# Weight slots of 6176 instead of 6144 bytes, weights 16 bytes inside, state-and-value tiles of 3328 instead of 3200 bytes

## The chip, the core and the metric

The kernel runs on one core of one Trainium2 chip. The metric is the device time of one execution in microseconds (us); a nanosecond is written ns. Engines are named as the profile names them: PE is the matrix engine (its matmuls), PEld its weight loads, DVE the vector engine, ACT the scalar engine, POOL the general one, and SP the engine that issues the DMAs.

## What is computed

A recurrent attention layer (4 batches, 8 heads, 768 steps, head size 48), and two MLPs behind it, all in float32:

```python
f = 1.0 / (1.0 + np.exp(-f_logit))
for t in range(S):
    state = f[:, :, t, :, None] * state + np.einsum('bhd,bhe->bhde', k[:, :, t], v[:, :, t])
    y[:, :, t] = np.einsum('bhd,bhde->bhe', q[:, :, t], state)
...
x = attn_out.transpose(0, 2, 1, 3).reshape(3072, 384)
h = x @ w_in;  g = np.maximum(h, 0.0) ** 2;                     x = g @ w_out     # first MLP, 384 -> 2048 -> 384
h = x @ w_in2; g = h * np.tanh(np.log1p(np.exp(h)));            return g @ w_out2 # second MLP, same sizes
```

## The kernel before

**Tiling.** The 3072 tokens are six blocks of 512. The hidden size of 2048 is sixteen chunks of 128, numbered fc. For each MLP and each block, `l1` (matmul at line 333) computes the hidden activations of one chunk and `l2` (line 344) adds that chunk's share to three accumulators. Each is a group of nine matmuls of 128x128 weights against 512 columns: three 128-column slices of the weights, times three products (high part of the weights with the high and the low part of the activations, low part of the weights with the high part). Every matmul of a group uses weights other than the one before it, so each has its own weight load (LDWEIGHTS). Six blocks, two MLPs, sixteen chunks and two projections make 384 groups, that is 3456 matmuls of 512 columns; the very last group is issued as 18 half-width matmuls by `last_l2` (line 840).

**Stages.** First comes a start of some 34 us with attention work alone. Then the first MLP runs with the attention of the later token blocks interleaved in PE's queue (short matmuls at lines 471, 486, 518, 525, 538 and others). From about 425 us on, PE does only the second MLP. In both MLPs PE's queue alternates the groups: `l1` of chunk fc, then `l2` of a chunk one or two back, then `l1` of the next. The order of the first part is written out in a table (`START`), and the rest by due times (`put`); neither is touched.

**Where the weights lie.** A weight tile holds, in each of 128 partitions, 1536 floats (6144 bytes): two halves (for `l1` and for `l2`), in each a high and a low part of 384 floats. All slices of 128 columns begin at multiples of 512 bytes inside the tile. Sixteen such slots, tags `w_0` to `w_15` of pool `wp`, hold the first MLP's weights: `load_w` (line 240) fetches the packed float64 bits into the slot, DVE and ACT take them apart into a `wbit` tile, and `w_hi` and `w_lo` (lines 275 and 281) write the high and low parts back into the slot. The first four of these slots in memory, `w_15` to `w_12`, serve earlier as input tiles of the attention (`early`). The second MLP's weights go through DRAM: `w2_back` (line 316) fetches chunks 5 to 15 into `w_0` to `w_10`, and chunk 4 into a slot `w_late` of pool `at2`; `w2_early` fetches the two halves of chunks 0 to 3 into tiles of the attention that are free by then (pool `lt`; table `EARLY`): the `l1` halves into `kn0`, `kn1`, `mv0`, `mv1`, the `l2` halves into `vs0` to `vs3`, the state-and-value tiles.

Tiles follow one another in memory by their sizes, in the order in which the pools are opened and the tags first used. That gives each tile's place in its partition; what is left over modulo 256 bytes is, before and after:

| tile | place modulo 256, before | after |
|---|---|---|
| weights in slots, in memory order `w_15`, `w_14`, `w_13`, `w_12`, `w_0` ... `w_9`, `w_11`, `w_10` | all 0 | 16, 48, 80, 112, 144, 176, 208, 240, and the same eight again |
| chunk 4 of the second MLP (`w_late`) | 0 | 16 |
| `l1` halves of chunks 0 to 3, second MLP (`kn`, `mv`) | all 0 | all 0 |
| `l2` halves of chunks 0 to 3, second MLP (`vs0` to `vs3`) | 0, 128, 0, 128 | all 0 |
| activations `x`, `gh`, `gl` (the moving operand of every group) | all 0 | all 0 |
| attention inputs `early` (begin of slots `w_15` to `w_12`) and `in` | 0 and 128 | 0, 32, 64, 96 and 128 |

Of the kernel before, what the change touches and what calls it, by code (L numbers as in the profile page):

```python
# [9 lines left out]
F32 = mybir.dt.float32  # L10
F32R = mybir.dt.float32r
U32 = mybir.dt.uint32
# [17 lines left out]
DM = 384  # L30
# [53 lines left out]
@with_exitstack  # L84
def attention_mlps(ctx: ExitStack, tc: tile.TileContext, qkf, vv, w1, w2, out):
    keep = ctx.enter_context(tc.tile_pool(name="keep", bufs=1))
    flag = keep.tile([1, 1], I32, name="flag")
    fast_path(tc, flag, qkf, vv, w1, w2, out)
    beyond = tc.nc.values_load(flag[0:1, 0:1], min_val=0, max_val=1)
    with tc.If(beyond > 0):  # L90
        stepwise_path(tc, qkf, vv, (w1, w2), out)
# [122 lines left out]
def fast_path(ctx: ExitStack, tc: tile.TileContext, flag, qkf, vv, w1, w2, out):  # L214
    nc = tc.nc
    V, A, G, T = nc.vector, nc.scalar, nc.gpsimd, nc.tensor
    const = ctx.enter_context(tc.tile_pool(name="const", bufs=1))
    wp = ctx.enter_context(tc.tile_pool(name="wp", bufs=1))
    bit_p = ctx.enter_context(tc.tile_pool(name="bit", bufs=3))
    lt = ctx.enter_context(tc.tile_pool(name="lt", bufs=1))  # L220
# [17 lines left out]
    xt, wt, raw, bits, hps, gt, accs, x2t = {}, {}, {}, {}, {}, {}, {}, {}  # L238

    def load_w(fc):  # L240
        t = wp.tile([128, 2 * DM, 2], U32, tag=f"w_{fc}", name=f"r_{fc}", bufs=1)
        nc.sync.dma_start(out=t.rearrange("p c w -> p (c w)"), in_=w1[fc].bitcast(U32))
        raw[fc] = t

    def w_abs(fc):
        b = bit_p.tile([128, 2 * DM], U32, tag="wbit", name="wbit")
# [25 lines left out]
    def halves(b):  # L272
        return b.bitcast(F32).rearrange("p (s c) -> p s c", s=2)

    def w_hi(fc):
        del raw[fc]
        w = wp.tile([128, 2, 2, DM], F32R, tag=f"w_{fc}", name=f"w_{fc}", bufs=1)
        A.activation(out=w[:, :, 0], in_=halves(bits[fc]), func=AF.Copy, scale=F_SCALE)
        wt[0, fc] = w

# [34 lines left out]

    def w2_back(fc):
        pool, tag = (late[0], "w_late") if fc < NL else (wp, f"w_{fc - NL}")
        w = pool.tile([128, 2, 2, DM], F32R, tag=tag, name=f"w_{fc}", bufs=1)
        for half in range(2):
            nc.sync.dma_start(out=w[:, half].bitcast(F32), in_=w2d[fc][half])  # L320
        wt[1, fc] = w
# [58 lines left out]

    def attention(at, at1):
        inp = [at1.tile([128, 3, 512], F32, name=f"in{i}") for i in range(2)]
        early = [wp.tile([128, 3, 512], F32, tag=f"w_{15 - i}", name=f"early{i}", bufs=1) for i in range(4)]

        def fkq(i):
            t = early[i - 2] if 2 <= i < 6 else inp[i % 2]
# [2 lines left out]
        def head(t):  # L389
            return t.rearrange("p (h t) -> p h t", h=H)  # L390

        vs = [lt.tile([128, 2 * DM + 32], F32, tag=f"vs{i}", name=f"vs{i}") for i in range(4)]
        mv = [lt.tile([128, 2, H, C], F32, tag=f"mv{i}", name=f"mv{i}") for i in range(2)]
        kns = [lt.tile([128, 2, H, D], F32, tag=f"kn{i}", name=f"kn{i}") for i in range(2)]
        idn = at1.tile([128, 128], F32, name="idn")
# [297 lines left out]
        for f in range(FC):  # L693
            if f >= 4:
                put(last + max(f - NL + 4, 1), 50, w2_back, f)
            for half in (0, 1):
                if f < 4:
                    put(last + EARLY[f][half][1] + 1, 50, w2_early, f, half)
                put(22 + 3 * f, 50, w2_load, f, half)
                put(23 + 3 * f, 58, w2_abs, f, half)  # L700
                put(25 + 3 * f, (62, 70)[half], w2_split, f, half)
            put(24 + 3 * f, 60, w2_bits, f)
# [29 lines left out]
        def finish():  # L732
            act_a(n1 - 1)
            act_b(n1 - 1)

        ops = (v_min, a_exp, a_ln, v_scan, a_dq, a_dk, v_q, v_k, v_end, v_fmin, m_a, m_t, v_mask, a_kn, m_y, m_u, a_y,
               m_x, y_dma, a_x, v_x, v_s, load_j, load_f, load_v, load_w, w_abs, w_shift, w_top, w_low, w_hi, w_lo, do_l1,
               do_l2, act_a, act_b, m_warm, eye_kn)
        ops = {f.__name__: f for f in ops}
# [17 lines left out]
    def phase1(at, at1):  # L757
        return attention(at, at1)
# [185 lines left out]
```

## Time and profile before

| | |
|---|---|
| median of 3 runs | 897.87 us (897.76 to 898.22) |
| the profiled execution, its own time | 899.2 us |
| its span, first to last instruction | 897.5 us |
| PE busy | 884.0 us, 99% of the span |
| PEld / DVE / ACT busy | 725.6 / 676.2 / 618.3 us |
| granted clock of PE | 0.999 of full speed, mean |

The profile is one execution. A matmul's busy time is modelled and overlaps the next one's, so the time that a matmul costs is read from the distance of starts, or from the chain of waits, which cuts the span into pieces that don't overlap and gives for each group of nine its length. A piece of the chain is named by engine, tile and line.

### The profile page before, as it was taken

The page shows a single profiled execution, that of the slowest core. Times are in us where ns is not written, and L with a number is a line of the kernel's source. Part 1 is how long each engine was busy: PE and PEld are TensorE (multiplying, and loading weights), DVE is VectorE, ACT ScalarE, POOL GpSimd, SP SyncE. Part 2 cuts the span into 40 slices and gives each one's busy share as a digit, 9 for nine tenths or more (in the row PEclk, how much of TensorE's full clock was granted, in tenths as well). Part 3 has the DMA queues.
Part 4 walks back from the last instruction along what each step waited for, and adds up shares of the span by engine and source line. Part 5 has one row for each costly group of instructions (what it writes and reads, how often), then busy time and mean ns, then how long its engine had stood idle before and what let it go on. Part 6 is the DMA issues. An engine that isn't in the chain of part 4 may idle for free.

```text
span 897.5 us, 15329 instructions
## 1 busy us (share of the span) xinstructions
PE 884.0 (99%) x5927; PEld 725.6 (81%) x5927; DVE 676.2 (75%) x1146; ACT 618.3 (69%) x1131; POOL 5.2 (1%) x21
## 2 busy tenths in 40 slices
PE   8999999999999999999999999999999999999997
PEld 7788888888787887888888888888888888888885
DVE  8999976876778877772222788888788888888785
ACT  8798776876787778764544566666666676666664
POOL 2000000000000000000000000000000000000000
PEclk9999999999999999999999999999999999999999
DMA  9922223455536454632453100200200200200001
GB/s 319 392 91 106 91 96 114 166 172 167 186 132 230 152 205 163 213 106 81 175 202 115 71 0 1 72 1 0 71 1 1 71 0 1 72 1 0 36 1 38
DMA packets 34735, 92.29 MB, mean 103 GB/s; under 512 B 5216, under 2 KB 11360, under 8 KB 34656
## 3 DMA queue, kind: packets, MB, share of 16 engines
q1 hardware_dynamic: 34656, 91.25, 29.4%
q8 instruction: 48, 0.79, 0.4%
q14 instruction: 31, 0.25, 0.1%
HBM read 66.06 MB, written 22.02 MB: 98 GB/s over the span
## 4 chain that ended last, share of the span: by engine, by line
PE 87%; ACT 4%; DVE 4%; DMA 2%; SPq 1%; issue 1%; ACTq 0%
PE h L333 41%; PE a L344 40%; PE y L525 2%; DMA ax<-ay 1%; PE tr L486 1%; PE aq L471 1%; PE y L518 1%; PE at L476 1%; ACT r L716 1%; PE uq L538 1%; DMA sr<-in_w_dram 1%; PE u L543 1%; DVE mv L449 0%; ACT r L715 0%; ACT gh L352 0%
## 5 line engine op out<-in xcount | busy, mean ns | idle before, releaser
L333 PE MATMUL h<-x,w 128*128 128x512 f32 x1728 | 425.5, 390 | 0.7 <-ACT x L602 0.4
L344 PE MATMUL a<-gh,w 128*128 128x512 f32 x1146 | 388.3, 394 | 0.0
L333 PEld LDWEIGHTS h<-x,w 128*128 128x128 f32 x1728 | 323.5, 188 | 70.4 <-DVE x L606 1.0
L344 PEld LDWEIGHTS a<-gh,w 128*128 128x128 f32 x1146 | 215.2, 188 | 46.0
L344 PE MATMUL a<-gl,w 128*128 128x512 f32 x573 | 223.6, 391 | 0.0
L782 ACT ACTIVATE e<-e 128x512 f32<-128x512 f32 x95 | 60.1, 632 | 117.5 <-DVE e L781 117.5
L344 PEld LDWEIGHTS a<-gl,w 128*128 128x128 f32 x573 | 107.7, 188 | 22.1 <-DVE gl L357 0.7
L357 DVE TENSOR_TENSOR gl<-r,gh 128x512 fp32r<-128x512 f32 x96 | 65.8, 686 | 78.8 <-ACT gh L352 76.7
L781 DVE TENSOR_SCALAR e<-h 128x512 f32<-128x512 f32 x95 | 65.7, 692 | 60.7 <-PE h L333 58.1
L715 ACT ACTIVATE r<-h 128x512 f32<-128x512 f32 x96 | 56.6, 590 | 49.0 <-PE h L333 48.6
L776 ACT ACTIVATE r<-u,cst 128x512 f32<-128x512 f32 x94 | 67.9, 723 | 8.7 <-DVE u L790 2.7
L790 DVE SCALAR_TENSOR_TENSOR u<-e 128x512 f32<-128x512 f32 x95 | 65.9, 694 | 10.0 <-ACT e L782 0.7
L357 DVE TENSOR_TENSOR gl<-g,gh 128x512 fp32r<-128x512 f32 x95 | 65.7, 692 | 0.0
L778 DVE TENSOR_TENSOR e<-h,u 128x512 f32<-128x512 f32 x94 | 64.3, 684 | 0.0
L785 DVE TENSOR_TENSOR g<-e,r 128x512 f32<-128x512 f32 x94 | 64.2, 683 | 0.0
L352 ACT ACTIVATE gh<-r 128x512 fp32r<-128x512 f32 x96 | 60.7, 633 | 3.1
L716 ACT ACTIVATE r<-r 128x512 f32<-128x512 f32 x96 | 60.7, 632 | 3.0
L352 ACT ACTIVATE gh<-g 128x512 fp32r<-128x512 f32 x95 | 60.1, 633 | 3.1 <-DVE g L809 0.8
L777 ACT ACTIVATE r<-r 128x512 f32<-128x512 f32 x94 | 59.5, 633 | 3.0
L606 DVE TENSOR_TENSOR x<-ax,x 128x384 fp32r<-128x384 f32 x16 | 8.9, 556 | 35.9 <-ACT x L602 35.9
L602 ACT ACTIVATE x<-ax 128x384 fp32r<-128x384 f32 x16 | 8.4, 525 | 38.5 <-DMA ax<-ay 38.3
L508 ACT ACTIVATE kn<-tr 64x192 f32<-64x192 f32 x88 | 28.4, 322 | 6.1 <-PE tr L486 5.2
(120 smaller groups left out, 729.2 us busy)
## 6 DMA issues: line engine op xcount, KB each, us to landing
in<-in_qkf_dram SPq DMA_DIRECT2D x18, 768.0 KB, 5.8
r<-in_w_dram SPq DMA_DIRECT2D x16, 768.0 KB, 9.6
sr<-in_w_dram SPq DMA_DIRECT2D x32, 384.0 KB, 3.5
w2d<-sw SPq DMA_DIRECT2D x32, 384.0 KB, 3.1
w<-w2d SPq DMA_DIRECT2D x32, 384.0 KB, 3.5
vs<-in_vv_dram SPq DMA_DIRECT2D x48, 96.0 KB, 5.6
x2d<-ot SPq DMA_DIRECT2D x18, 256.0 KB, 2.1
x<-x2d SPq DMA_DIRECT2D x6, 768.0 KB, 5.1
```

Source lines behind the costliest of these rows:

```text
L333: T.matmul(out=ps, lhsT=w[:, k * 128:(k + 1) * 128], rhs=x[:, s, k], start=(i == 0), stop=(i == 8))
L344: T.matmul(out=acc[m], lhsT=w[:, m * 128:(m + 1) * 128], rhs=gx, start=(fc == 0 and i == 0), stop=(fc == FC - 1 and i == 2))
L352: A.activation(out=gh, in_=g, func=AF.Copy)
L357: V.tensor_tensor(out=gl, in0=g, in1=gh.bitcast(F32), op=ALU.subtract)
L716: A.activation(out=r, in_=r, func=AF.Square)
L776: A.activation(out=r, in_=u, func=AF.Ln, bias=two)
L777: A.activation(out=r, in_=r, func=AF.Exp, scale=-1.0)
L778: V.tensor_tensor(out=e, in0=hp, in1=u, op=ALU.mult)
L781: V.tensor_scalar(out=e2, in0=ps, scalar1=20.0, scalar2=None, op0=ALU.min)
L782: A.activation(out=e2, in_=e2, func=AF.Exp)
L785: V.tensor_tensor(out=g, in0=e, in1=r, op=ALU.mult)
L790: V.scalar_tensor_tensor(out=u2, in0=e2, scalar=2.0, in1=e2, op0=ALU.add, op1=ALU.mult)
```

## The change

Three kinds of tile grow, and nothing else is edited.

- A weight slot is 1544 floats (6176 bytes) instead of 1536. The packed bits and the attention's `early` inputs still lie at the slot's begin; the split weights lie 4 floats (16 bytes) inside it (`four`). This holds for `load_w`, `w_hi`, `w2_back` (with `w_late`) and `early`.
- The state-and-value tiles `vs` are 832 floats (3328 bytes, 13 times 256) instead of 800 (3200).
- Because `w_late` is the first tile of `at2`, that pool's other tiles (`x2`, `e`, `u`, `g`) lie at 32 instead of 0 modulo 256.

On every engine the instructions, their order, and the semaphores that each waits for are the same, row by row.

```diff
     def load_w(fc):
-        t = wp.tile([128, 2 * DM, 2], U32, tag=f"w_{fc}", name=f"r_{fc}", bufs=1)
-        nc.sync.dma_start(out=t.rearrange("p c w -> p (c w)"), in_=w1[fc].bitcast(U32))
-        raw[fc] = t
+        t = wp.tile([128, 4 * DM + 8], U32, tag=f"w_{fc}", name=f"r_{fc}", bufs=1)[:, 0:4 * DM]
+        nc.sync.dma_start(out=t, in_=w1[fc].bitcast(U32))
+        raw[fc] = t.rearrange("p (c w) -> p c w", w=2)
...
+    def four(t):
+        return t[:, 4:4 * DM + 4].rearrange("p (s h c) -> p s h c", s=2, h=2)
+
     def w_hi(fc):
         del raw[fc]
-        w = wp.tile([128, 2, 2, DM], F32R, tag=f"w_{fc}", name=f"w_{fc}", bufs=1)
+        w = four(wp.tile([128, 4 * DM + 8], F32R, tag=f"w_{fc}", name=f"w_{fc}", bufs=1))
...
     def w2_back(fc):
         pool, tag = (late[0], "w_late") if fc < NL else (wp, f"w_{fc - NL}")
-        w = pool.tile([128, 2, 2, DM], F32R, tag=tag, name=f"w_{fc}", bufs=1)
+        w = four(pool.tile([128, 4 * DM + 8], F32R, tag=tag, name=f"w_{fc}", bufs=1))
...
-        early = [wp.tile([128, 3, 512], F32, tag=f"w_{15 - i}", name=f"early{i}", bufs=1) for i in range(4)]
+        early = [wp.tile([128, 4 * DM + 8], F32, tag=f"w_{15 - i}", name=f"early{i}", bufs=1) for i in range(4)]
+        early = [t[:, 0:4 * DM].rearrange("p (j c) -> p j c", j=3) for t in early]
...
-        vs = [lt.tile([128, 2 * DM + 32], F32, tag=f"vs{i}", name=f"vs{i}") for i in range(4)]
+        vs = [lt.tile([128, 2 * DM + 64], F32, tag=f"vs{i}", name=f"vs{i}") for i in range(4)]
```

## Rows read from the trace of the kernel before

**Rows 1.** The page's head, its busy times by engine, and PE's granted clock by slice

```profile
span 897.5 us, 15329 instructions
PE 884.0 (99%) x5927; PEld 725.6 (81%) x5927; DVE 676.2 (75%) x1146; ACT 618.3 (69%) x1131; POOL 5.2 (1%) x21
PEclk9999999999999999999999999999999999999999
```

**Rows 2.** The chain that ended last, by engine and line

```profile
PE 87%; ACT 4%; DVE 4%; DMA 2%; SPq 1%; issue 1%; ACTq 0%
```

**Rows 3.** Waits of PE for others, the longest: total, times, longest in us

```profile
PE warm L613 <- DVE cst L622: 1.8, 1, 1.8
PE aq L471 <- PE h L333: 1.0, 1, 1.0
```

**Rows 4.** Chain from 500 us: start, length in us, what; xN are matmuls

```profile
500.95 2.04 PE h L333 x9
502.99 2.04 PE a L344 x9
505.03 2.05 PE h L333 x9
507.08 2.11 PE a L344 x9
509.19 2.09 PE h L333 x9
511.27 2.04 PE a L344 x9
513.31 2.05 PE h L333 x9
515.36 2.11 PE a L344 x9
517.47 2.09 PE h L333 x9
519.55 2.04 PE a L344 x9
```

**Rows 5.** The last two such pairs of twelve in the whole chain

```profile
835.15 2.11 PE a L344 x9
837.26 2.09 PE h L333 x9
843.43 2.11 PE a L344 x9
845.54 2.09 PE h L333 x9
```

**Rows 6.** Weight loads by form, 425 to 890 us: count, busy us, mean ns

```profile
L333 PEld LDWEIGHTS h<-x,w 128*128 128x128 f32 x1009 | 189.3, 188 | 40.1
```

**Rows 7.** Timeline of PE, half-width matmuls of the last group: start, us, xcount

```profile
889.47 0.40 PE L840 MATMUL a<-gh,w 128*128 128x256 f32 x2
889.71 0.40 PE L840 MATMUL a<-gl,w 128*128 128x256 f32 x2
```

**Rows 8.** Chain from 205 us: a restart behind attention matmuls

```profile
209.22 2.04 PE h L333 x9
211.26 0.62 PE aq L471 x32
211.88 0.53 PE tr L486 x4
212.42 2.10 PE a L344 x9
214.52 2.05 PE h L333 x9
```

**Rows 9.** Whole chain, first and last of some 40 groups from 2.09 us, 42 to 425 us

```profile
54.06 2.27 PE a L344 x9
...
417.09 2.27 PE a L344 x9
```

**Rows 10.** DMA issues: count, KB each, median us from issue to landing

```profile
w<-w2d SPq DMA_DIRECT2D x32, 384.0 KB, 3.5
in<-in_qkf_dram SPq DMA_DIRECT2D x2, 512.0 KB, 6.5
early<-in_qkf_dram SPq DMA_DIRECT2D x2, 512.0 KB, 7.9
```

**Rows 11.** Windows, second MLP: us, busy (xcount) of PE, PEld, DVE, ACT, POOL, clock, DMA

```profile
660.00:890.00 230.00, 229.90 (x1019) 189.41 (x1018) 188.59 (x299) 152.95 (x243) 0.00 (x0) 1.00 0.05 18
```

## The prediction

> **What bounds the kernel now.** I read the page's busy times first [rows 1]: PE is busy 884.0 of 897.5 us, and its clock stands at its upper level (2.4 GHz) in every slice. The shares of the chain [rows 2] say the same: 87% of it is PE, and the longest single wait of PE for another engine is 1.8 us, at the start [rows 3]. So the time is nearly the sum of what PE's matmuls cost one after the other, and a change moves it by what it does to the distance between them. That distance is read in the chain by groups of nine. In the settled state a group takes 2.04 us [rows 4], or 226.7 ns a matmul. 512 columns at 2.4 GHz are 213.3 ns, so 13.3 ns of each matmul are something else. The weight loads run beside the matmuls, 188 ns each [rows 6], which fits into 226.7 ns.
>
> The change alters no instruction, no order and no wait. It alters where things lie. So the question is whether the trace shows a distance that depends on place. It does. At 507.08 and 515.36 us stand groups of 2.11 us, and behind each an `l1` group of 2.09 us [rows 4]. Counting `l1` and `l2` groups from the begin of the second MLP, the two of 2.11 us are the `l2` groups of chunks 1 and 3 of the first block, whose weights lie in `vs1` and `vs3`, at 128 modulo 256 bytes. Those of chunks 0 and 2, in `vs0` and `vs2` at 0, take 2.04 us. The pairs come back in all six blocks, twelve in all [rows 4, 5]. Nothing else sets these tiles apart: the same line, form, moving operands and engines, and no wait. The group behind each has its weights at 0 and is still slower by 0.05 us, so what the place upsets takes a group to settle. Lengths of 2.10 and 2.27 us show behind interruptions by attention matmuls, though the weights are at 0 there [rows 8, 9].
>
> My reading is that a matmul's stream of columns and the weight load beside it get into each other's way at some relative places, and that a stream of groups, all with weights and columns at 0, settles into a rhythm in which they don't.
>
> **The change part by part.** The sum starts from the profiled execution's 899.2 us, 1.3 us above the median of 897.87; the differences are then applied to the median.
>
> *The `vs` tiles* go from 0, 128, 0, 128 to 0 everywhere. Alone, this returns twelve times 0.07 us (2.11 against 2.04) and twelve times 0.045 us (2.09 against 2.045): 1.4 us less.
>
> *The weight slots.* 384 groups of nine; 48 of them (chunks 0 to 3 of the second MLP, six blocks, two projections) keep weights at 0. The other 336 get weights at 16, 48, 80 and so on up to 240. The columns stay at 0, and consecutive groups never have the same place: chunk 5 reads at 48, then `l2` of chunk 3 at 240, chunk 6 at 80, `l2` of chunk 4 at 16. No row shows these places. Bounds for one group: as the settled one, nothing; as the one at 128, 0.07 us more. Below nothing: the 13.3 ns a matmul could shrink, 0.12 us a group, but the last group speaks against that. Its half-width matmuls start 0.24 us apart in twos [rows 7], 120 ns each, and 256 columns are 106.7 ns: 13.3 ns again, so this looks like a fixed price of one matmul and not a collision that grows with the stream. I take 0.045 us a group, the row of the group that follows another place, since here every group follows another place, whatever its own place costs: 336 x 0.045 = 15.1 us. At 0.07 us it would be 23.5 us.
>
> *Groups at 0 that follow a shifted one.* In each block of the second MLP five of the eight groups at 0 do (`l1` of chunks 0 and 1, later `l2` of chunk 2 and 3, `l1` of chunk 2): 30 x 0.045 = 1.4 us more.
>
> *What is unsettled already.* Some 40 groups in the chain between 42 and 425 us take 2.09 us or more [rows 9], because they follow a restart [rows 8]. They can't be upset twice: 40 x 0.045 = 1.8 us to take off the sum.
>
> *DMAs into shifted slots.* The inputs in `in` (at 128) land in 6.5 us and those in `early` (at 0) in 7.9 us, of the same size [rows 10]: no sign that a transfer wants to begin at a multiple of 256. The loads of the second MLP's weights land in 3.5 us and PE waits for none of them [rows 3, 10]. I take 0, and 1 us as the upper bound, for the start, where the first MLP's weights are awaited.
>
> *DVE and ACT* write and read tiles at other places (weights at 16, `e`, `u`, `g` at 32). In the second MLP's last 230 us they are busy 188.6 and 153.0 us [rows 11], so some slowing hides there; what it would cost without that cover is at most the 41 us that DVE has idle turned into waits, which needs DVE slower by a fifth. 0, and 1 us upward.
>
> Sum: 15.1 + 1.4 - 1.4 - 1.8 = 13.3 us more. The profiled execution becomes 912.5 us and the median 897.87 + 13.3 = 911.2 us. Upper bound: 23.5 + 1.4 - 1.4 - 2.8 (40 x 0.07) + 2 = 22.7 us, 920.6 us.
>
> A page of the Trainium skill speaks against this whole term. "SBUF — State Buffer", section "Who interferes with whom", says that only the port pair shared by DVE and GpSimd causes contention, and that PE and ACT never wait on anyone. "TensorE: Matmul & The Clock Gate", section "Step-by-step: what each phase is for", adds that loading the next weights takes no read bandwidth from the running matmul, since PE has two independent read ports. By these the place of a weight can't cost anything and the time stays 897.9 us. The trace disagrees: 2.11 against 2.04 us, with the place as the only difference [rows 4].
>
> **The rivals.** *Faster, because spread places settle sooner.* The restarts take long to settle although all lies at 0 [rows 8, 9]; it may be the equal places of weights and columns that make this rhythm hard to reach, and any place but 0 and 128 may be free of it. Then the twelve pairs (1.4 us) and the 40 restarts (40 x 0.06, 2.10 against 2.04) go: 3.8 us less, 894.1 us. Against it speaks that the one other place in the trace is worse, and that every stretch at 0 does settle. It decides from the point at which a group at, say, 48 that follows one at 240 takes 2.04 us.
>
> *Much faster, because the 13.3 ns are the collision.* Weights and columns begin at the same place in every settled matmul; if the extra 13.3 ns are the price of just that, moving the weights takes them away: up to 3456 x 13.3 = 46 us, half of it 23 us, 875 us. For it: two streams through the same places collide equally often in a half-width matmul, so that row doesn't exclude it. Against it: at 128 it grew instead of shrinking.
>
> *No change.* Only a place half-way round (128) upsets the rhythm, or the twelve pairs are slow for a reason that I don't see. Then the slots do nothing, and at most the 1.4 us come back: 896.5 to 897.9 us.
>
> **How the numbers follow.** About 0.2% (1.8 us) is what a measurement here can tell from no change. Forecast, slower by some 3 to 23 us: 0.58. No change: 0.14. Faster through quicker settling, around 894 us: 0.20. Much faster: 0.08. So faster 0.28, same 0.14, slower 0.58. The range reaches from 893, which takes in the quicker settling, to 921, the upper bound; it leaves out the much faster case and what lies above. The forecast's own range is 901 to 921.
>
> **What would show it.** In the chain of the changed kernel, groups between 425 and 505 us, all 2.04 us now, would read 2.08 to 2.11, some of them differing by place: slots at 112 and 144 slower than those at 16 and 240. The `l2` groups of chunks 1 and 3 of the second MLP would lose their pattern of 2.11 and 2.09 us against their neighbours. PE's waits for others would stay as short as now, and the weight loads at 188 ns. I am wrong if groups with shifted weights take 2.04 us (no change, or faster if the restarts shorten too), or less than 2.04 us, which would make the 13.3 ns a matter of place.

## The result, and the profile after

The changed kernel takes 907.26 us (906.89 to 907.40) against 898.05 us: ratio 1.0102, 95% interval 1.0085 to 1.0120, that is 9.2 us slower. The profiled span grows from 897.5 to 905.5 us. Of the kernels below, the one with all weights at 128 had one execution of 2260.83 us at PE's full clock, for which no cause is known, beside three of 912.46 to 912.93 us: its ratio is of the three, its median of all four.

The page's head and the shares of the chain of the changed kernel, beside [rows 1] and [rows 2]:

```profile
span 905.5 us, 15329 instructions
PE 893.4 (99%) x5927; PEld 727.0 (80%) x5927; DVE 676.0 (75%) x1146; ACT 619.2 (68%) x1131; POOL 5.2 (1%) x21
...
PE 96%; DVE 2%; DMA 0%; issue 0%; ACT 0%
```

PE has 9.4 us more of busy time with as many instructions. DVE and ACT have the same as before within 1 us. In the chain PE's share has grown from 87% to 96%: where the chain ran through ACT, DVE and DMAs before, almost all of it now runs through PE. The matmuls became longer and partly grew into time in which PE had waited.

The chain of the changed kernel early in the second MLP, beside [rows 4] (start, length in us, what). By the count of groups the second MLP starts at 492.6 us in the kernel before and at 496.2 us in this one. The 425 us under "Stages" are the end of the attention's matmuls only; from there to 492.6 us PE does the last groups of the first MLP.

```profile
510.79 2.04 PE a L347 x9
512.83 2.04 PE h L336 x9
514.87 2.04 PE a L347 x9
516.91 2.04 PE h L336 x9
518.95 2.04 PE a L347 x9
521.00 2.08 PE h L336 x9
523.07 2.10 PE a L347 x9
525.17 2.10 PE h L336 x9
527.27 2.10 PE a L347 x9
529.37 2.06 PE h L336 x9
531.43 2.07 PE a L347 x9
533.50 2.10 PE h L336 x9
535.60 2.09 PE a L347 x9
537.69 2.10 PE h L336 x9
```

The group at 510.79 us is `l2` of chunk 1, which took 2.11 us before; it now lies at 0 and takes 2.04 us. From 521.00 us on the groups read their weights at 176, 16, 208, 144, 240, 176, 16, 208 and 48, and take 2.06 to 2.10 us. Two shifted groups stand ahead of them, at 512.83 us (place 16) and 516.91 us (place 144), and take 2.04 us like the groups at 0 around them. The same two places take 2.10 us at 523.07 and 527.27 us. So the length of a group follows from its place and from what ran ahead of it.

Sum the distances of starts of all adjacent 512-column matmuls in the two traces, leaving out the restarts' first steps and the waits. The part over the settled 226.7 ns is 2.0 us before and 8.1 us after in the first MLP, 1.5 and 5.6 us in the second: 10.2 us more. The span grew by 8.0 us.

### The profile page after: what moved, and what is told of

Same layout as the page of the kernel before. It is cut to its first block, busy times and chain, and to the rows that moved or that the text cites. A ratio compares the mean times of both kernels' runs of the same rounds, so it can differ in the third digit from the quotient of the medians.

```text
span 905.5 us, 15329 instructions
## 1 busy us (share of the span) xinstructions
PE 893.4 (99%) x5927; PEld 727.0 (80%) x5927; DVE 676.0 (75%) x1146; ACT 619.2 (68%) x1131; POOL 5.2 (1%) x21
## 4 chain that ended last, share of the span: by engine, by line
PE 96%; DVE 2%; DMA 0%; issue 0%; ACT 0%
PE a L347 44%; PE h L336 44%; PE y L529 2%; PE tr L490 1%; PE aq L475 1%; PE y L522 1%; PE uq L542 1%; PE at L480 1%; PE u L547 1%; DVE mv L453 0%; DVE es L438 0%; DMA in<-in_qkf_dram 0%; PE a L844 0%; DVE vs L596 0%; DVE x L610 0%
## 5 line engine op out<-in xcount | busy, mean ns | idle before, releaser
L336 PE MATMUL h<-x,w 128*128 128x512 f32 x1728 | 431.1, 394 | 0.3 <-DVE x L610 0.3
```

Of the source, the lines that this page charges most:

```text
L336: T.matmul(out=ps, lhsT=w[:, k * 128:(k + 1) * 128], rhs=x[:, s, k], start=(i == 0), stop=(i == 8))
```

## The experiments

The ratios below are each against runs of the kernel before on the same chip beside them, with medians of 898.5 to 898.8 us.

**Each half of the change alone.** The first edit is the state-and-value tiles:

```diff
-        vs = [lt.tile([128, 2 * DM + 32], F32, tag=f"vs{i}", name=f"vs{i}") for i in range(4)]
+        vs = [lt.tile([128, 2 * DM + 64], F32, tag=f"vs{i}", name=f"vs{i}") for i in range(4)]
```

> One half of the change alone: the state-and-value tiles of 3328 bytes, so that all weights of the second MLP lie at 0 modulo 256; the weight slots stay at 6144 bytes. If the place of the weights against the columns sets the distance of matmuls, the twelve pairs of 2.11 and 2.09 us become 2.04 us and the time falls by about 1.4 us, to some 896.6 us against 898.05, with no group of nine over 2.05 us in the second MLP apart from the one behind the flag's matmuls. If place has nothing to do with it, the time stays at 898.0 us and the pairs stay.

Measured: 897.01 us, ratio 0.9985 (0.9976 to 0.9994), 1.3 us faster (0.5 to 2.2). The chain of this kernel, at the place of [rows 4]:

```profile
505.95 2.04 PE a L344 x9
507.99 2.04 PE h L333 x9
510.03 2.04 PE a L344 x9
512.07 2.04 PE h L333 x9
514.11 2.04 PE a L344 x9
516.15 2.04 PE h L333 x9
```

The groups of 2.11 and 2.09 us are gone. By the starts, the second MLP's 1.5 us over the settled distance fall to nothing, which is the price that the prediction gave them. No kernel of the study is faster than this one by more than the spread of its runs, and it beats both the kernel before and the changed one. A further 256 bytes make no difference: `vs1` and `vs3` now begin an odd multiple of 256 behind `vs0`, and settle as it does.

The second run has the new slots with the old state-and-value tiles:

```diff
-        vs = [lt.tile([128, 2 * DM + 64], F32, tag=f"vs{i}", name=f"vs{i}") for i in range(4)]
+        vs = [lt.tile([128, 2 * DM + 32], F32, tag=f"vs{i}", name=f"vs{i}") for i in range(4)]
```

> The other half alone: slots of 6176 bytes with the weights 16 bytes inside, state-and-value tiles as before (0, 128, 0, 128). If the slots carry the loss, the time is that of the change, 907 us, or up to 1.4 us above it, since the l2 groups of chunks 1 and 3 stay at 128. If the loss came from the longer state-and-value tiles, it is 898 us.

Measured: 908.17 us, ratio 1.0105 (1.0089 to 1.0120). The slots carry the whole loss.

**One place for all weights.** To tell the place itself from the change of place, every weight of both MLPs is put at one place P while the columns stay at 0, with the slots 6144 bytes apart as before. For 128:

```diff
-    wsum = const.tile([128, 3 * FC + 24], F32, name="wsum")[:, 0:3 * FC]
+    wsum = const.tile([128, 3 * FC + 24 + 32], F32, name="wsum")[:, 0:3 * FC]
...
-        w = pool.tile([128, 2, 2, DM], F32R, tag=tag, name=f"w_{fc}", bufs=1)
+        pad = 32 if fc < NL else 0
+        w = pool.tile([128, 4 * DM + (64 if fc < NL else 0)], F32R, tag=tag, name=f"w_{fc}", bufs=1)
+        w = w[:, pad:pad + 4 * DM].rearrange("p (s h c) -> p s h c", s=2, h=2)
...
-        vs = [lt.tile([128, 2 * DM + 32], F32, tag=f"vs{i}", name=f"vs{i}") for i in range(4)]
+        vs = [lt.tile([128, 2 * DM + 64], F32, tag=f"vs{i}", name=f"vs{i}") for i in range(4)]
...
-        kns = [lt.tile([128, 2, H, D], F32, tag=f"kn{i}", name=f"kn{i}") for i in range(2)]
+        kns = [lt.tile([128, 2 * DM + 32 * i], F32, tag=f"kn{i}", name=f"kn{i}") for i in range(2)]
+        kns = [t[:, 0:2 * DM].rearrange("p (y h e) -> p y h e", y=2, h=H) for t in kns]
```

> All weights of both MLPs at 128 modulo 256, the columns at 0: slots 6144 bytes apart as before, with one pad ahead of them and one behind, and state-and-value tiles of 3328 bytes. Theory A (the relative place itself costs): every group of nine takes some 2.10 us, 233 ns a matmul, and the time is about 898 + 384 x 0.06 = 921 us. Theory B (a change of place from group to group costs, and any constant place settles): groups of 2.04 us, about 896 to 898 us. In between: a constant place settles after one or two groups, and only the restarts become longer.

Measured: 912.87 us, ratio 1.0155 (1.0137 to 1.0174), slower than the changed kernel. The chain of this kernel:

```profile
508.44 2.09 PE a L346 x9
510.52 2.10 PE h L335 x9
512.62 2.09 PE a L346 x9
514.71 2.09 PE h L335 x9
516.80 2.09 PE a L346 x9
518.89 2.10 PE h L335 x9
```

No group settles, though nothing changes from group to group. So the change of place isn't needed: a constant place costs. It costs less than the 921 us expected, 0.05 us a group instead of 0.06, and the expectation took nothing off for the 3.5 us that were unsettled already. The weight loads show 188 ns each here as in the kernel before, so the lengthening doesn't appear in their recorded time. The starts of the single matmuls show it: distances of 232, 228, 230, 233, 241, 232 and 231 ns come round again and again to the end of the kernel.

**Weights and columns moved together.** The pad stands ahead of the slots alone, so that all behind it moves too:

```diff
-    wsum = const.tile([128, 3 * FC + 24], F32, name="wsum")[:, 0:3 * FC]
+    wsum = const.tile([128, 3 * FC + 24 + 32], F32, name="wsum")[:, 0:3 * FC]
```

> Weights and columns both at 128 modulo 256 (one pad of 128 bytes ahead of all slots; state-and-value tiles of 3328 bytes). If it is the place of the weights against the columns, this is the same as both at 0: some 896.6 us and groups of 2.04 us. If it is the weights' own place in memory, every group takes some 2.10 us and the time is about 921 us, whatever the columns do. If transfers or the vector and scalar engines want tiles that begin at multiples of 256 bytes, it is slower without longer groups of matmuls.

Measured: 897.05 us, ratio 0.9982 (0.9973 to 0.9992). The chain of this kernel:

```profile
506.22 2.04 PE a L344 x9
508.26 2.04 PE h L333 x9
510.30 2.04 PE a L344 x9
512.34 2.04 PE h L333 x9
```

The weights lie at the same place in memory as in the run before and the groups are settled. What counts is where the weights lie against the columns. Nor do transfers, DVE and ACT cost anything at 128, since all their tiles behind the pad lie there in this kernel; with all of them at 32 (`const16` below) they cost nothing either.

**The other places.** The pads are changed, nothing else. Two of these runs are not what their label and the text on record say: tiles are placed at multiples of 32 bytes, so the pads of 16 and 240 bytes were rounded up. `const16` has weights and columns both at 32 (distance 0; `w_late`, with its own offset, at distance 16, and settled there too, with 0 ahead of it), `const240` has weights at 0 and columns at 32 (distance 224; `w_late` at 240). They are read as that below. So no run holds a constant distance of 16 or of 240.

> All weights at 16 modulo 256, columns at 0, otherwise as the run with all at 128. In the changed kernel groups at 16 behind one at 0 took 2.04 us, and behind one at 80 or 176 took 2.10 us. If there is a band of places round 0 in which the rhythm settles, and 16 is in it, this is some 897 us; if every place but 0 keeps cycling, some 912 us.

> All weights at 64 modulo 256, columns at 0. If a place outside a band round 0 never settles, it costs as 128 does: about 912 us, groups of 2.08 to 2.11 us through both MLPs. If the cost grows with the distance from 0, it lies half-way: about 905 us. If the conflict repeats every 64 bytes, 897 us.

> All weights at 192 modulo 256, columns at 0: the mirror of 64. If only the distance from 0 counts, the same time as the run at 64. If it matters which of the two streams is ahead, another: in the changed kernel groups at 176 took 2.07 us and those at 80 2.09 us, which points to the places below 256 as the cheaper side, some 900 to 908 us.

> All weights at 240 modulo 256, columns at 0: 16 bytes ahead of 0. In the changed kernel groups at 240 took 2.04 us behind one at 0 and 2.05 to 2.07 us behind others. If this place settles, and sooner after a restart than 0 does, the time is below that of the kernel with all at 0, 895 to 897 us; if it settles as 0 does, 897 us; if not, some 912 us.

> All weights at 32 modulo 256, columns at 0. Measured so far with one place for all: 0 settles at 226.7 ns a matmul, 64 gives 233.3, 128 gives 232.4, 192 gives 228.9 ns. If the settling place is a narrow one at 0, 32 costs as 64 does, some 917 us; if it is a band on the side of 0 where the weights lie ahead of the columns, 897 us.

> All weights at 96 modulo 256, columns at 0. Between 64 (917.7 us) and 128 (912.9 us): if the cost follows the distance smoothly, some 915 us.

> All weights at 160 modulo 256, columns at 0. Between 128 (912.9 us) and 192 (902.6 us): if the cost follows the distance smoothly, some 908 us; if there is a second settling place on this side, as groups at 144 of 2.04 us in the changed kernel hint, some 897 us.

The results, by the distance of the weights from the columns modulo 256. The matmuls between 500 and 880 us are the count in that window of the second MLP; the ns are the mean distance of starts of adjacent 512-column matmuls from 425 us on, worked out from the trace. The last stretch of the first MLP is in that mean, which mixes places in the rows of before and of the change:

| distance, run | median us | ratio to before (95%) | matmuls in the 380 us | ns a matmul |
|---|---|---|---|---|
| 0 (`vs_alone`) | 897.01 | 0.9985 (0.9976 to 0.9994) | 1680 | 226.7 |
| 0, both at 128 (`shift_all128`) | 897.05 | 0.9982 (0.9973 to 0.9992) | 1680 | 226.7 |
| 0, both at 32 (`const16`) | 897.79 | 0.9995 (0.9981 to 1.0009) | 1680 | 226.7 |
| 32 | 915.97 | 1.0191 (1.0174 to 1.0208) | 1632 | 233.3 |
| 64 | 917.70 | 1.0205 (1.0179 to 1.0231) | 1633 | 233.3 |
| 96 | 918.43 | 1.0214 (1.0197 to 1.0231) | 1626 | 234.3 |
| 128 | 912.87 | 1.0155 (1.0137 to 1.0174) | 1639 | 232.4 |
| 160 | 916.17 | 1.0195 (1.0177 to 1.0212) | 1633 | 233.3 |
| 192 | 902.57 | 1.0050 (1.0036 to 1.0064) | 1664 | 228.9 |
| 224 (`const240`) | 915.05 | 1.0188 (1.0170 to 1.0207) | 1635 | 233.0 |
| before (0, with two groups a block at 128) | 898.05 | | 1674 | 227.4 |
| the change (16 to 240 in turn) | 907.26 | 1.0102 (1.0085 to 1.0120) | 1657 | 230.2 |

Two of these windows, of the kernels at 160 and at 192 (stretch, length, busy and count of PE, PEld, DVE, ACT, POOL, clock, DMA):

```profile
500.00:880.00 380.00, 380.00 (x1633) 305.40 (x1632) 303.31 (x474) 246.35 (x386) 0.00 (x0) 1.00 0.07 24
```

```profile
500.00:880.00 380.00, 380.00 (x1664) 311.57 (x1663) 311.01 (x487) 252.54 (x396) 0.00 (x0) 1.00 0.07 24
```

PE is busy all the time and its clock is at the upper level in both; there are 31 matmuls more in the second. Of the seven distances tried outside 0 none settles, and neither distance nor direction orders them: 96 is the worst, 192 by far the mildest. Smooth growth with the distance was wrong, and so was a second settling place at 160: the times expected for 64, 96 and 160 were all too low. That 192 is the cheaper side, read from the changed kernel's groups at 176, was right. In the time of `const64` there is something else besides: the mean clock of its profiled execution was 0.87 in the first 40 us, so part of them at the lower level, and its MLP began later. Its two executions with a mean clock of 0.998 took 915.64 and 916.05 us. The 233.3 ns are not touched by that.

```profile
0.00:40.00 40.00, 35.68 (x461) 33.46 (x462) 33.82 (x60) 28.38 (x63) 5.34 (x21) 0.87 0.96 333
```

**Two places in turn.** The `l1` and `l2` halves of a slot are put 128 bytes apart, so that the queue runs through 0, 128, 128, 0, 0, 128, 128:

```diff
-        w = wp.tile([128, 2, 2, DM], F32R, tag=f"w_{fc}", name=f"w_{fc}", bufs=1)
+        w = halved(wp, f"w_{fc}", fc)
...
+    def halved(pool, tag, fc):
+        t = pool.tile([128, 4 * DM + 32], F32R, tag=tag, name=f"w_{fc}", bufs=1)
+        t = bass.AP(tensor=t.tensor, offset=t.offset, ap=[t.ap[0], [2 * DM + 32, 2], [DM, 2], [1, DM]])
+        return t
```

> The l1 and l2 halves of a slot 128 bytes apart modulo 256 (slots of 6272 bytes), columns at 0, state-and-value tiles as before: PE's queue then runs through places 0, 128, 128, 0, 0, 128, 128 and so on; 180 of the 384 groups are at 128. If a group's own place alone counts, those 180 cost 0.055 us each: some 898 + 9.9 = 908 us, and the others stay at 2.04 us. If a group at 0 that follows one at 128 pays too, as the pairs of the kernel before show, some 90 more groups cost 0.05 us: 912 us, hardly less than with all weights at 128 (912.9 us).

Measured: 906.10 us, ratio 1.0078 (1.0061 to 1.0095), some 7 us above before; below both expectations and nearer to the first. The chain of this kernel, with the places 128, 128, 0, 0, 128, 128, 0, 0:

```profile
526.92 2.10 PE a L349 x9
529.02 2.09 PE h L338 x9
531.11 2.04 PE a L349 x9
533.15 2.05 PE h L338 x9
535.20 2.10 PE a L349 x9
537.30 2.09 PE h L338 x9
539.39 2.04 PE a L349 x9
541.43 2.05 PE h L338 x9
```

Both groups at 128 pay, the one that changes the place and the one that keeps it. The groups at 0 behind them take 2.04 us: by their starts two matmuls are late (233 and 230 ns), then they are settled. Behind a single group at 128, as in [rows 4], the group at 0 needs ten matmuls for that; at the begin of each block this kernel has such a place too and shows the same 2.09 us there:

```profile
510.32 2.11 PE a L349 x9
512.42 2.09 PE h L338 x9
514.51 2.04 PE a L349 x9
```

So at 128 a group pays chiefly for its own place; what a predecessor leaves behind depends on the order and is small here. At other places the order can count for more: the changed kernel's groups at 16 and 144 pay nothing behind groups at 0.

## Why the prediction came out right, and where its terms were off

The forecast was 13.3 us slower, 911.2 us; measured are 9.2 us and 907.26 us, inside the range. Point by point:

*The `vs` tiles, 1.4 us less.* Right: 1.3 us in the run of that half alone (0.5 to 2.2), and the twelve pairs are gone.

*The weight slots, 15.1 us.* Right in kind, and near in size. In the changed kernel's trace the 512-column matmuls with shifted weights lie 13.5 us in sum above 226.7 ns a step, 0.038 us a group of nine in the second MLP and 0.044 us in the first. But the reason for which I chose 0.045 us out of 0 to 0.07 was wrong. I charged each group for following another place. The runs with one place for all show groups that follow the same place and pay 0.02 us (192) to 0.07 us (96), and the run with two places in turn shows followers at 0 that pay 0.01 us. The price is chiefly that of a group's own distance from the columns, and in part that of the order. It averaged 0.04 us in the changed kernel because 40 of its 335 shifted groups of nine are settled behind certain predecessors (as those at 512.83 and 516.91 us), and because places at 176 and 240 cost less in its order. That 0.045 us, read from a group at 0, came so near to the mean of eight other places is luck.

*Groups at 0 that follow a shifted one, 1.4 us.* Mis-sized: 0.2 us in the trace. It is the same mistake. The pair in [rows 4] was the only row of a follower, and it is one of the few orders in which the follower pays.

*What was unsettled already.* I took off 1.8 us for the restarts and 1.4 us for the pairs; the trace of before has 2.0 and 1.5 us. Right.

*What the sum left out.* These terms as measured give 13.7 - 3.5 = 10.2 us, and the span grew by 8.0. I had taken the time as the sum of PE's matmuls; but PE did wait a little, and part of these waits is gone where the matmuls are longer. By the starts, the first steps of groups behind a wait or a restart add up to 1.4 us less, and the stretches of attention matmuls between groups to 0.7 us less. PE's idle time between 40 and 425 us fell from 1.8 us to 0.65 us by the windows (the second row is of the changed kernel):

```profile
40.00:425.00 385.00, 383.19 (x3365) 309.99 (x3365) 300.06 (x549) 288.45 (x590) 0.00 (x0) 1.00 0.44 148
```

```profile
40.00:425.00 385.00, 384.35 (x3356) 308.92 (x3355) 298.89 (x546) 288.28 (x589) 0.00 (x0) 1.00 0.44 148
```

About 1.0 of the 1.4 us is one `l1` group of the first MLP. In the kernel before it waited for its columns, which ACT and DVE made from a late transfer; in the changed kernel the same group follows `l2` without a wait. The chains of before, then of the changed kernel:

```profile
348.20 3.33 DMA ax<-ay
...
351.72 0.53 ACT x L602
...
352.27 0.57 DVE x L606
...
352.88 2.14 PE h L333 x8
```

```profile
351.97 2.10 PE a L347 x9
354.07 2.10 PE h L336 x9
```

The chain's share of PE, 87% before [rows 2] and 96% after, had shown that other engines held parts of the way; I read it as a sign that PE bounds the kernel and gave those parts no term.

*DMAs, DVE and ACT, nothing.* Right: `w<-w2d` lands in 3.6 us against 3.5 [rows 10], DVE and ACT are as busy as before, and with all tiles moved by 128 nothing is lost.

*The sign by place.* Half right. By the starts, a group of the changed kernel takes in the mean over the settled 2.04 us: 0.013 us more at 240, 0.031 at 176, 0.038 at 144, 0.045 at 16, 0.048 at 80, 0.052 at 208, 0.057 at 112 and 0.059 at 48: 112 is dear and 240 cheap as forecast, but 144 is cheaper than 16. PE's longest wait stayed 1.8 us and a weight load 188 ns, as forecast.

*The rivals.* Quicker settling at spread places: wrong; seven constant distances outside 0 don't settle at all. The 13.3 ns as the collision itself: no run brought the mean below 226.7 ns, at eight distances, so none of these places gets anything of them back. No change: wrong. What speaks against it is against the two pages of the Trainium skill named in the prediction as well: with the columns at 0 and the weights moved to 128 a matmul takes 232.4 instead of 226.7 ns, and with both moved together 226.7 ns. That the two read ports themselves disturb each other is not shown by that.

Why a distance of 0 settles and others don't, and why the rhythm at 128 has seven steps, is not shown. That the weight load and the stream of columns meet in reading the same memory fits all runs; no run took loads away to prove it. Not every matmul needs a load of its own, other than the section on tiling says: of each three in a group the first two use the same 128x128 weights, the high part, with the high and with the low part of the columns. The trace has a load for each all the same (PE and PEld both 5927).

## What to carry to other kernels

Where matmuls follow one another without a gap, look at the distance of their starts for one and the same form; if it differs between tiles, compare where the weights and the moving operand lie modulo 256 bytes. Here both at the same place was the best of eight distances, worth about 3% of a matmul's time against six of them, so here the tiles between them should be padded to multiples of 256 bytes. Whether a constant distance below 32 bytes settles is open. A second tile size that breaks this (3200 bytes) cost 1.3 us unseen, since PE showed as busy all the same.

## What the runs showed of the hardware

The distance of matmuls depends on the relative place of weights and columns: 226.7 ns at 0, 228.9 at 192, 232.4 to 234.3 ns at the six other distances tried, with no order by size. Where it doesn't settle it repeats: 231, 232, 237 ns at 160; 231 and 236 ns in turn in some stretches at 64 and 233 to 234 ns throughout in others. And it has a memory over groups: weights at 16 and at 144 ran at 226.7 ns a matmul when the groups ahead of them lay at 0, and at some 233 ns a few groups later, while the constant places nearest to 144 (128 and 160) never got below 232 ns in the mean. Behind attention matmuls, too, it takes some ten matmuls until 226.7 ns are back: from 212.51 us in the kernel before 232, 229, 234, 235, 225, 230, 236, 229, 232, 231, then 227 ns. The 128x512 matmul's extra 13.3 ns over its 512 columns at 2.4 GHz stayed in all runs.
